# Pooling of k and v from the second batch on: accumulating transfers add the upper four of eight rows

## The chip, the cores and the metric

The kernel runs on one core of one Trainium2 chip. The metric is the device time of one execution in microseconds (us). Fewer is better.

## The reference, cut to what matters

Three stages follow one another, all in float32.

```
k_p = k.reshape(B, H, Sp, 8, D).mean(axis=3)      # k, v: (4, 8, 576, 64), Sp = 72
v_p = v.reshape(B, H, Sp, 8, D).mean(axis=3)
attn = softmax(q @ k_p^T / sqrt(64));  x = attn @ v_p        # 2304 tokens x 512
x = (silu(xn @ w_gate) * (xn @ w_val)) @ w_out               # xn = x / rms(x) * g, d_ff 1536
out = (x @ w_a) * (x @ w_b) @ w_out2                         # d_ff 1536
```

What is changed is the first two lines: each mean is over 8 rows of 64 numbers that lie side by side in memory, so that one pooled row is made of 512 contiguous numbers (2 KB). A batch has 576 such groups for k and 576 for v (8 heads of 72).

## The kernel before, in words

Tokens are worked on in tiles of 512, 256, 512, 512 and 512. In the first tile attention, the conversion of the weights and the first feed-forward run side by side; `FIRST` and `SECOND` (lines 32 to 52) are lists of tokens that give the order in which the steps are written for the first two tiles, and a list scheduler then places the instructions on each engine by its own estimate of when they are ready. Once placed, every engine works in that order, and an instruction that waits holds up all behind it on its engine. The same holds for SP, which issues all transfers. Each weight is loaded in 512 KB pieces (`st`, four buffers), scaled by ACT (L589, L590), given its sign by DVE (L596, L599) and completed by POOL (L606) into `wf`; a matrix product needs a rounded weight `wh` (ACT, L620) and its rest `wl` (POOL or DVE, L621). Products of the first tile are L791 (g and v) and L814 (`acc`); of later tiles L649 and L662. The bank of v is a single one: the next product v can't begin before DVE has read the last one (`ht`, L805 in the first tile, L1235 later).

`prep_steps(b)` pools k and v of batch b. `load` (L158) brings a piece of two chunks, each 72 rows (one head of k) or 128 rows (v) by 512 numbers; v ends in a chunk of 64 rows, so a batch has 7 pieces. Buffers are `kv`, two of them (the first batch has others besides). `pool_to` (L174) sums a chunk by `reduce_sum` over the 8 rows (DVE, L189, one instruction a chunk) or, where a token has an exclamation mark, a piece by three halving additions on POOL (L180 twice, L183), and then calls `load` for the next piece. In batch 1 seven chunks are summed by DVE and three pieces by POOL; in batches 2 and 3 DVE sums all 13 chunks. The pooled keys `kp` are transposed by PE (L210) and copied to `KB`; the pooled values `vp` are spread into `vm` (L228, L244) and split (`vh`, `vl`, L253, L254). The scores are L318, their maximum and difference L327 and L328, and `el` (L380) is the rest of the transposed weights of attention, which the product xT (L399) needs.

After the attention of the last tile, which is over at about 300 us, PE works through the rest of the first feed-forward and the whole second one.

Of the kernel before, what the change touches and what calls it, by code (L numbers as in the profile page):

```python
# [8 lines left out]
F32 = mybir.dt.float32  # L9
# [3 lines left out]
I64 = mybir.dt.int64  # L13
AF = mybir.ActivationFunctionType
ALU = mybir.AluOpType
AX = mybir.AxisListType

P = 128
# [45 lines left out]
def attention_moe_moe2(  # L64
# [14 lines left out]
    nc = tc.nc  # L79
    B, H, S, D = q.shape  # L80
    NT, DM = out.shape
    FF = w_gate.shape[1]
    POOL = 8
    SP = S // POOL
# [4 lines left out]
    NV = 5  # L89
# [12 lines left out]
    at_p = attn.enter_context(tc.tile_pool(name="at", bufs=2, side="right"))  # L102
# [9 lines left out]
    for t0, n in starts(TILES1):  # L112
# [9 lines left out]
        out=mask, in_=mask, pattern=[[P, NV], [-SP, H]], compare_op=ALU.is_ge,  # L122
# [3 lines left out]
        out=mask, in_=mask, pattern=[[-P, NV], [SP, H]], compare_op=ALU.is_ge,  # L126
# [3 lines left out]
    for i in range(2):  # L130
        t = const.tile([P, NP, 2 * SP], F32, tag=f"KB{i}", name=f"KB{i}")
# [10 lines left out]
    def att_bank(name, tag=None):  # L142
        if tag is not None:
            pass
        else:
            tag = boot["banks"].pop(0) if boot["banks"] else "att"
        return ps.tile([P, 512], F32, tag=tag, name=name, bufs=2 if tag == "att" else 1)

    def prep_steps(b):
        kf = k[b].rearrange("h (sp r) d -> (h sp) (r d)", r=POOL)  # L150
        vf = v[b].rearrange("h (sp r) d -> (h sp) (r d)", r=POOL)
        tail = HK - (NV - 1) * P
        pieces = [(kf[c * SP:(c + 2) * SP], SP) for c in range(0, H, 2)]
        pieces += [(vf[c * P:(c + 2) * P], P) for c in range(0, NV - 1, 2)]
        pieces += [(vf[(NV - 1) * P:], tail)]
        queue = []

        def load():  # L158
            if not pieces:
                return  # L160
            src, rows = pieces.pop(0)
            i = len(pieces)
            if boot["on"] and i not in (1, 4):
                t = st_p.tile([P, 512], I64, tag="st", name=f"kv_{b}_{i}")
            else:
                t = at_p.tile([P, 512], I64, tag="kv", name=f"kv_{b}_{i}", bufs=2)
            t = t.bitcast(F32).rearrange("p (c x) -> p c x", c=2)
            if rows == tail:
                nc.sync.dma_start(out=t[:rows, 0], in_=src)
            else:  # L170
                nc.sync.dma_start(out=t[:rows], in_=src.rearrange("(c p) x -> p c x", p=rows))
            queue.append((t, rows))

        def pool_to(dst, c0, on_pool=False):  # L174
            t, rows = queue.pop(0)
            nc_ = 1 if rows == tail else 2
            if on_pool:
                v4 = t[:rows, :nc_].rearrange("p c (r d) -> p c r d", r=POOL)
                for half in (4, 2):
                    nc.gpsimd.tensor_add(  # L180
                        v4[:, :, :half, :], v4[:, :, :half, :], v4[:, :, half:2 * half, :]
                    )
                nc.gpsimd.tensor_add(  # L183
                    dst[:rows, c0:c0 + nc_, :], v4[:, :, 0, :], v4[:, :, 1, :]
                )
                load()
                return
            for c in range(nc_):
                nc.vector.reduce_sum(  # L189
                    out=dst[:rows, c0 + c, :],  # L190
                    in_=t[:rows, c].rearrange("p (r d) -> p d r", r=POOL),
                    axis=AX.X,
                )
            load()

        box = {}

        def k_pool(c):
            if c == 0:
                box["kp"] = sm_p.tile([SP, H, D], F32, tag="kp", name=f"kp_{b}")  # L200
            pool_to(box["kp"], c, boot["alt"])

        def v_pool(c):
            pool_to(vp, c, boot["on"] or boot["alt"])

        def k_transpose():
            kb = KB[b % 2]
            kp, bank = box["kp"], att_bank(f"kT_{b}")
            for p in range(NP):
                nc.tensor.transpose(  # L210
                    bank[:, p * SP:(p + 1) * SP],
                    kp[:, 2 * p:2 * p + 2, :].rearrange("p a d -> p (a d)"),
                    ident[:SP, :SP],
                )
            for hh in range(2):
                rows = slice(hh * D, (hh + 1) * D)
                dst = kb[rows, :, hh * SP:(hh + 1) * SP]
                src = bank[rows, :NP * SP].rearrange("p (a s) -> p a s", a=NP)
                if hh == 0 and b == 0:
                    nc.scalar.mul(dst, src, 1.0 / POOL)  # L220
                else:
                    nc.vector.tensor_scalar_mul(dst, src, 1.0 / POOL)

        def v_mask():
            vm = at_p.tile([P, NP, 2, P], F32, tag="vh", name=f"vm_{b}")
            VM[b] = vm
            for pr in range(NP):
                nc.gpsimd.tensor_mul(  # L228
                    vm[:, pr].rearrange("p c (a d) -> p c a d", a=2),
                    vp[:, pr:pr + 2, :].unsqueeze(2).to_broadcast([P, 2, 2, D]),  # L230
                    mask[:, pr:pr + 2, 2 * pr:2 * pr + 2].unsqueeze(3).to_broadcast([P, 2, 2, D]),
                )

        def v_split(half):
            if half == 0:
                VH[b] = at_p.tile([P, NP, 2, P], F32R, tag="vh", name=f"vh_{b}")
                VL[b] = at_p.tile([P, NP, 2, P], F32R, tag="vl", name=f"vl_{b}")
            if b in VM:
                vm = VM[b][:, 2 * half:2 * half + 2].rearrange("p a c d -> p (a c d)")
            else:  # L240
                vm = ev_p.tile([P, 512], F32, tag="ev", name=f"vm_{b}_{half}")
                for i in range(2):
                    pr = 2 * half + i
                    nc.vector.tensor_mul(  # L244
                        vm[:, i * 256:(i + 1) * 256].rearrange("p (c a d) -> p c a d", c=2, a=2),
                        vp[:, pr:pr + 2, :].unsqueeze(2).to_broadcast([P, 2, 2, D]),
                        mask[:, pr:pr + 2, 2 * pr:2 * pr + 2].unsqueeze(3).to_broadcast(
                            [P, 2, 2, D]
                        ),
                    )  # L250
            dst_h = VH[b][:, 2 * half:2 * half + 2].rearrange("p a c d -> p (a c d)")
            dst_l = VL[b][:, 2 * half:2 * half + 2].rearrange("p a c d -> p (a c d)")
            nc.scalar.copy(dst_h, vm)  # L253
            nc.vector.tensor_sub(dst_l, vm, dst_h.bitcast(F32))  # L254

        loads = [load] * (6 if b == 0 else 2)
        steps = [lambda c=c: k_pool(c) for c in range(0, H, 2)]
        steps += [lambda c=c: v_pool(c) for c in range(0, NV, 2)]
        steps += [k_transpose]
        if b < 2:  # L260
            steps += [v_mask]
        if b > 0:
            steps += [lambda h=h: v_split(h) for h in range(2)]
        return loads, steps
# [416 lines left out]
    A = [score_steps(u) for u in range(NU)]  # L681
    V = [value_steps(u, dest(u)) for u in range(NU)]
    loads, prep = zip(*(prep_steps(b) for b in range(B)))

    nc.sync.dma_start(out=gneg, in_=rms_g.rearrange("(c p) -> p c", p=P))
# [615 lines left out]
```

## Time and profile before

| what | us |
|---|---|
| median of 3 runs (1028.54, 1029.00, 1031.03) | 1029.0 |
| the execution that was profiled | 1029.57 |
| its span, first to last instruction | 1027.8 |
| PE busy (95% of the span) | 978.7 |
| DVE busy (62%) | 638.3 |
| POOL busy (41%) | 417.3 |

PE is TensorE's matmuls, PEld its weight loads, DVE is VectorE, ACT ScalarE, POOL GpSimd, SP the engine that issues transfers. Times of a timeline are microseconds from the span's start. What stands in square brackets behind a row is how long the engine was idle before it, and what it waited for.

### The profile page before, as it was taken

How to read it: one execution, taken by the hardware profiler on the slowest of the kernel's cores; microseconds unless marked ns; L12 is line 12 of the kernel's file. 1: busy time of each engine (PE TensorE's matmuls, PEld its weight loads, DVE VectorE, ACT ScalarE, POOL GpSimd, SP SyncE). 2: the span in 40 equal slices, each digit the busy share in tenths (PEclk: the TensorE clock that was granted, in tenths of full speed). 3: DMA queues.
4: the chain of work that ended last, by engine and by line, in shares of the span. 5: the costliest groups of instructions: out<-in, count | busy, mean ns of one | idle time of the engine just before them, and what ended most of it. 6: DMA issues, size and time to landing. Idle time of an engine off the chain costs nothing. (4 is left out here: it accounts for less than half of the span.)

```text
span 1027.8 us, 13784 instructions
## 1 busy us (share of the span) xinstructions
PE 978.7 (95%) x4988; PEld 846.3 (82%) x4988; DVE 638.3 (62%) x994; ACT 463.4 (45%) x874; POOL 417.3 (41%) x332
## 2 busy tenths in 40 slices
PE   4978999989899999999999999999999999999998
PEld 3766666788788887888788889999999999888886
DVE  6898966997843756363627759766676665322221
ACT  2855662565454536444436545434444434331211
POOL 5476672546443434344357620533344332310000
PEclk8799999989999999999999999999999999999999
DMA  8556543330100002000102033444443434643431
GB/s 220 163 175 193 174 134 102 102 91 1 41 1 21 1 1 62 1 1 1 41 24 80 28 125 108 144 135 147 138 144 130 134 128 167 213 141 118 138 112 72
DMA packets 82803, 101.55 MB, mean 99 GB/s; under 512 B 24112, under 2 KB 63024, under 8 KB 82736
## 3 DMA queue, kind: packets, MB, share of 16 engines
q1 hardware_dynamic: 82736, 100.69, 31.5%
q8 instruction: 39, 0.64, 0.3%
q14 instruction: 28, 0.23, 0.1%
HBM read 73.93 MB, written 26.74 MB: 98 GB/s over the span
## 5 line engine op out<-in xcount | busy, mean ns | idle before, releaser
L621 POOL TENSOR_TENSOR wl<-wf,wh 128x512 fp32r<-128x512 f32 x156 | 214.1, 1382 | 236.0 <-ACT wh L620 234.0
L620 ACT CAST wh<-wf 128x512 fp32r<-128x512 f32 x168 | 102.0, 618 | 77.3 <-PE v L649 28.8
L1095 DVE TENSOR_TENSOR hl<-hf,hh 128x768 fp32r<-128x768 f32 x36 | 34.4, 961 | 95.7 <-ACT hh L1094 95.6
L1117 PE MATMUL o<-woh,hl 128*128 128x512 f32 x216 | 85.8, 397 | 0.0
L1117 PE MATMUL o<-woh,hh 128*128 128x512 f32 x216 | 85.0, 394 | 0.0
L1117 PE MATMUL o<-wol,hh 128*128 128x512 f32 x216 | 84.7, 392 | 0.0
L606 POOL TENSOR_TENSOR w<-w,st 128x512 int32<-128x512 int32 x24 | 31.9, 1329 | 115.4 <-DVE w L599 114.3
L662 PE MATMUL acc<-hh,wl 128*128 128x512 f32 (+1 forms) x192 | 70.6, 368 | 5.7 <-ACT hh L1238 5.7
L649 PE MATMUL v<-xh,wl 128*128 128x512 f32 (+1 forms) x192 | 72.7, 379 | 1.1 <-DVE ht L1235 0.9
L649 PE MATMUL g<-xh,wl 128*128 128x512 f32 (+1 forms) x192 | 71.4, 372 | 0.0
L662 PE MATMUL acc<-hl,wh 128*128 128x512 f32 (+1 forms) x192 | 70.1, 368 | 0.5 <-DVE hl L1239 0.3
L649 PE MATMUL g<-xh,wh 128*128 128x512 f32 (+1 forms) x192 | 70.6, 368 | 0.0
L1094 ACT CAST hh<-hf 128x768 fp32r<-128x768 f32 x36 | 29.8, 834 | 90.2 <-PE o L1117 82.5
L649 PE MATMUL g<-xl,wh 128*128 128x512 f32 (+1 forms) x192 | 70.2, 366 | 0.0
L649 PE MATMUL v<-xl,wh 128*128 128x512 f32 (+1 forms) x192 | 70.0, 365 | 0.0
L649 PE MATMUL v<-xh,wh 128*128 128x512 f32 (+1 forms) x192 | 69.8, 363 | 0.0
L662 PE MATMUL acc<-hh,wh 128*128 128x512 f32 (+1 forms) x192 | 69.7, 364 | 0.0
L606 POOL TENSOR_TENSOR wf<-wf,st 128x512 int32<-128x512 int32 x36 | 53.0, 1477 | 38.8 <-DVE wf L599 16.6
L1235 DVE TENSOR_TENSOR ht<-ht,v 128x512 f32<-128x512 f32 (+1 forms) x48 | 29.6, 616 | 48.0 <-PE v L649 42.5
L1024 ACT COPY p<-X 128x384 f32<-128x384 f32 x36 | 17.3, 480 | 90.1 <-PE X L1016 90.1
L1227 ACT ACTIVATE ht<-g 128x512 f32<-128x512 f32 (+1 forms) x48 | 26.1, 545 | 63.8 <-PE g L649 54.5
L1239 DVE TENSOR_TENSOR hl<-ht,hh 128x512 fp32r<-128x512 f32 (+1 forms) x48 | 43.0, 895 | 14.6 <-ACT hh L1238 13.7
(208 smaller groups left out, 2772.5 us busy)
## 6 DMA issues: line engine op xcount, KB each, us to landing
hf<-h SPq DMA_DIRECT2D x36, 384.0 KB
st<-in_moe_w_out_dram SPq DMA_DIRECT2D x24, 512.0 KB
h<-u SPq DMA_DIRECT2D x36, 192.0 KB
h<-p SPq DMA_DIRECT2D x36, 192.0 KB
st<-in_moe_w_gate_dram SPq DMA_DIRECT2D x12, 512.0 KB
st<-in_moe_w_val_dram SPq DMA_DIRECT2D x12, 512.0 KB
st<-in_moe_w_a_dram SPq DMA_DIRECT2D x12, 512.0 KB
st<-in_moe_w_b_dram SPq DMA_DIRECT2D x12, 512.0 KB
```

The source lines that it names most:

```text
L606: nc.gpsimd.tensor_tensor(out=bits, in0=bits, in1=low, op=ALU.add)
L620: nc.scalar.copy(wh, wf[ph, f, i])
L621: (nc.vector if boot["alt"] else nc.gpsimd).tensor_sub(wl, wf[ph, f, i], wh.bitcast(F32))
L649: nc.tensor.matmul(bank[:, :n], w[:, c, :], x[:, c, cols], start=(i == 0), stop=(i == 3 * KD - 1),)
L662: nc.tensor.matmul(accs[c][:, cols], w[:, c, :], x[:, :n], start=(f == 0 and i == 0 and cols.start == 0), stop=(f == NF - 1 and i == 2),)
L1024: nc.scalar.copy(t, src[:, :HALF])
L1094: nc.scalar.copy(hh, hf)
L1095: nc.vector.tensor_sub(hl, hf, hh.bitcast(F32))
L1117: nc.tensor.matmul(accs[i], x[:, sub], y, start=(f == 0 and j == 0), stop=(f == NF - 1 and j == 2),)
L1227: act = nc.scalar.activation(out=ht[:, :m], in_=gb[:, :m], func=AF.Silu)
L1235: nc.vector.tensor_mul(ht[:, :m], ht[:, :m], vb[:, :m])
L1239: low = nc.vector.tensor_sub(hl[:, :m], ht[:, :m], hh.bitcast(F32)[:, :m])
```

## The change

From batch 1 on (batch 0 stays as it was) k and v come in four groups rather than seven pieces: two of four heads of k, one of four chunks of v, and the rest of v. Of each group two transfers are made. SP brings the lower four of the eight rows (`r = 0`, 1 KB of each 2 KB), and when these have landed, a transfer issued by POOL brings the upper four and adds them in memory to the lower ones (`accum_op`). A chunk then has 256 numbers a row instead of 512, so that `reduce_sum` goes over four rows, and POOL makes two additions a piece instead of three. There are still two `kv` buffers, each now of four chunks. A table gives the turns of `load` at which each transfer is issued.

```diff
+        groups = [(kf[c * SP:(c + 4) * SP], 4, SP) for c in range(0, H, 4)]
+        groups += [(vf[:(NV - 1) * P], NV - 1, P), (vf[(NV - 1) * P:], 1, tail)]
+        held, turn = {}, [0]
+
+        def issue(g, r):
+            src, cnt, rows = groups[g]
+            if r == 0:
+                t = at_p.tile([P, 512], I64, tag="kv", name=f"kv_{b}_{g}", bufs=2)
+                held[g] = t.bitcast(F32).rearrange("p (c x) -> p c x", c=4)
+            (nc.gpsimd if r else nc.sync).dma_start(
+                out=held[g][:rows, :cnt],
+                in_=src.rearrange("(c p) x -> p c x", p=rows)[:, :, r * 256:(r + 1) * 256],
+                **({"accum_op": ALU.add} if r else {}),
+            )
+            if r:
+                queue.extend((held[g][:, c:c + 2], rows) for c in range(0, cnt, 2))
+
         def load():
+            if b > 0:
+                for g, r in (
+                    [(0, 0), (1, 0)], [(0, 1), (1, 1)], [], [(2, 0)], [], [(3, 0), (2, 1), (3, 1)],
+                    [], [], [],
+                )[turn[0]]:
+                    issue(g, r)
+                turn[0] += 1
+                return
...
+            n_r = POOL if b == 0 else POOL // 2
             if on_pool:
-                v4 = t[:rows, :nc_].rearrange("p c (r d) -> p c r d", r=POOL)
-                for half in (4, 2):
+                v4 = t[:rows, :nc_].rearrange("p c (r d) -> p c r d", r=n_r)
+                for half in (4, 2)[-(n_r // 4):]:
...
-                    in_=t[:rows, c].rearrange("p (r d) -> p d r", r=POOL),
+                    in_=t[:rows, c].rearrange("p (r d) -> p d r", r=n_r),
```

Lines below the new code have numbers that are 26 higher in the kernel after: L189 is L215, L180 is L206, L596 and L599 are L622 and L625, L606 is L632, L621 is L647, L805 is L831. The new transfers are all L167.

The scheduler places things anew. Three places show what moves. The first is on DVE in batch 1, at about 44 to 55 us of the span before; `kp` are the pooled keys, `br` and `by` the small steps to the reciprocal root of the second half of the first tile, `dg` its result. Before:

```order
L478 TENSOR_SCALAR ba_472<-sq_413 128x4
L189 TENSOR_REDUCE kp_605<-kv_6_568 72x64
L481 TENSOR_SCALAR br_473<-ba_472 128x4
L189 TENSOR_REDUCE kp_605<-kv_6_568 72x64
L636 TENSOR_TENSOR xl<-xf_296,xh 128x2x256 x2
L485 TENSOR_SCALAR br_473<-br_473 128x4
```

And after, further down:

```order
L517 TENSOR_TENSOR by_474<-br_473 128x4
L215 TENSOR_REDUCE kp_607<-kv_0_568 72x64
L518 TENSOR_TENSOR by_474<-by_474,ba_472 128x4
L625 SCALAR_TENSOR_TENSOR wf_0_2_562<-st_2_0_433,wf_0_2_562 128x512
L519 SCALAR_TENSOR_TENSOR br_473<-by_474,br_473 128x4
L831 TENSOR_TENSOR ht<-ht,v 128x256
L490 TENSOR_SCALAR dg_487<-ident,br_473 128x128 x2
L215 TENSOR_REDUCE kp_607<-kv_0_568 72x64
```

Of the two reductions that stood ahead of `dg` one is left there, later in the chain, and the other stands behind it.

The second place is again on DVE, at about 152 to 161 us, where the keys of batch 2 come in; `ht` is the read that frees the bank of v. Before:

```order
L599 SCALAR_TENSOR_TENSOR wf_0_11_1434<-st_11_2_1317,wf_0_11_1434 128x512
L410 TENSOR_TENSOR ss_1217<-ss_1217,sq_3_1314 128x256
L805 TENSOR_TENSOR ht<-ht,v 128x512
L478 TENSOR_SCALAR ba_1396<-sq_1393 128x4
L481 TENSOR_SCALAR br_1397<-ba_1396 128x4
```

After:

```order
L625 SCALAR_TENSOR_TENSOR wf_0_11_1431<-st_11_2_1314,wf_0_11_1431 128x512
L436 TENSOR_TENSOR ss_1214<-ss_1214,sq_3_1311 128x256
L215 TENSOR_REDUCE kp_1590<-kv_1_970 72x64 x4
L831 TENSOR_TENSOR ht<-ht,v 128x512
L504 TENSOR_SCALAR ba_1393<-sq_1390 128x4
L507 TENSOR_SCALAR br_1394<-ba_1393 128x4
```

Four reductions of the second group of keys of batch 2 now stand ahead of `ht`; before, the first reduction of batch 2 stood eighteen rows behind it.

The third place is on POOL in the same stretch; `DMA` rows are the accumulating transfers of batch 2. Before:

```order
L621 TENSOR_TENSOR wl_1364<-wf_0_11_1331,wh_1363 128x512
L606 TENSOR_TENSOR wf_0_11_1434<-wf_0_11_1434,st_11_2_1317 128x512
L621 TENSOR_TENSOR wl_1422<-wf_0_0_240,wh_1421 128x512
L621 TENSOR_TENSOR wl_1471<-wf_0_11_1350,wh_1470 128x512
L621 TENSOR_TENSOR wl_1570<-wf_0_1_435,wh_1569 128x512
```

After:

```order
L647 TENSOR_TENSOR wl_1361<-wf_0_11_1328,wh_1360 128x512
L632 TENSOR_TENSOR wf_0_11_1431<-wf_0_11_1431,st_11_2_1314 128x512
L167 DMA kv_0_968<-in_k_dram 72x4x256
L167 DMA kv_1_970<-in_k_dram 72x4x256
L647 TENSOR_TENSOR wl_1419<-wf_0_0_240,wh_1418 128x512
L647 TENSOR_TENSOR wl_1468<-wf_0_11_1347,wh_1467 128x512
L167 DMA kv_2_1609<-in_v_dram 128x4x256
L167 DMA kv_3_1637<-in_v_dram 64x256
L647 TENSOR_TENSOR wl_1567<-wf_0_1_435,wh_1566 128x512
```

Four transfers have come in between, two of them ahead of the first `wl` of the second tile.

## Rows read from the trace of the kernel before

**Rows 1.** Page, part 1: busy us, share of the span, instructions.

```profile
PE 978.7 (95%) x4988; PEld 846.3 (82%) x4988; DVE 638.3 (62%) x994; ACT 463.4 (45%) x874; POOL 417.3 (41%) x332
```

**Rows 2.** Table by stretch; after the times PEclk is the granted clock.

```profile
87.25:91.70 4.45, 4.45 (x13) 3.48 (x13) 4.42 (x6) 2.14 (x4) 2.29 (x2) 0.62 0.55 184
186.40:209.66 23.26, 18.23 (x148) 17.41 (x146) 20.84 (x28) 13.59 (x27) 13.42 (x10) 0.96 0.30 82
209.66:214.50 4.84, 4.84 (x22) 4.84 (x23) 4.84 (x7) 2.04 (x7) 2.55 (x2) 0.50 0.20 58
300.00:1000.00 700.00, 695.23 (x3496) 616.38 (x3495) 393.30 (x615) 297.77 (x561) 249.73 (x190) 1.00 0.28 91
```

**Rows 3.** Lines 189 and 180: durations of one, least, median, most.

```profile
L189 DVE TENSOR_REDUCE kp<-kv x26: 995/1060/1128, 6.1 to 220.1; 72x64 f32<-72x512 f32 x26
...
L180 POOL TENSOR_TENSOR kv<-kv x14: 717/1010/1722, 9.0 to 85.1; 72x512 f32<-72x512 f32 x3, 72x256 f32<-72x256 f32 x3, 128x512 f32<-128x512 f32 x3, 128x256 f32<-128x256 f32 x3
```

**Rows 4.** Timeline of DVE, two contiguous reductions: start, duration, engine, line.

```profile
109.20 0.44 DVE L327 TENSOR_REDUCE m<-sc 128x4 f32<-128x288 f32 x1
...
115.07 1.34 DVE L339 TENSOR_REDUCE sum<-e 128x16 f32<-128x1152 f32 x1
```

**Rows 5.** Page, part 3: the one queue that moves data, packets, MB, share.

```profile
q1 hardware_dynamic: 82736, 100.69, 31.5%
```

**Rows 6.** Timeline of SP, then of ACT: one weight load and its first reader.

```profile
146.37 0.34 SPq L571 DMA_DIRECT2D st<-in_moe_w_out_dram  x1
...
149.66 0.68 ACT L589 ACTIVATE wf<-st 128x512 f32<-128x512 f32 x1 [0.87 <-DMA st<-in_moe_w_out_dram]
```

**Rows 7.** Timeline of DVE, 44 to 56 us: in the first batch with new pooling.

```profile
44.56 1.09 DVE L189 TENSOR_REDUCE kp<-kv 72x64 f32<-72x512 f32 x1
...
48.21 0.16 DVE L491 TENSOR_TENSOR by<-br 128x4 f32<-128x4 f32 x1
...
49.97 1.29 DVE L491 TENSOR_TENSOR by<-br 128x4 f32<-128x4 f32 x1
51.18 0.68 DVE L599 SCALAR_TENSOR_TENSOR wf<-st,wf 128x512 int32<-128x512 int32 x1
...
54.76 0.83 DVE L464 TENSOR_SCALAR dg<-ident,br 128x128 f32<-128x128 f32 x2
```

**Rows 8.** Timeline of POOL, the gap in the same stretch.

```profile
49.78 1.46 POOL L606 TENSOR_TENSOR wf<-wf,st 128x512 int32<-128x512 int32 x1 [4.20 <-DVE br L493]
```

**Rows 9.** Timeline of PE, its waits for DVE between 55 and 88 us.

```profile
55.65 0.70 PE L472 MATMUL rb<-dg,ones 128*128 128x256 f32 x2 [2.00 <-DVE dg L464]
...
76.98 0.47 PE L791 MATMUL v<-xh,wl 128*128 128x512 f32 x1 [1.43 <-DVE ht L805]
...
87.25 0.50 PE L791 MATMUL v<-xh,wl 128*128 128x512 f32 x1 [2.79 <-DVE ht L805]
```

**Rows 10.** Timeline of DVE, then of POOL and PE, around 156 us.

```profile
160.02 0.69 DVE L805 TENSOR_TENSOR ht<-ht,v 128x512 f32<-128x512 f32 x1 [4.14 <-PE v L791]
...
155.56 1.49 POOL L606 TENSOR_TENSOR wf<-wf,st 128x512 int32<-128x512 int32 x1
...
161.19 0.39 PE L791 MATMUL v<-xh,wl 128*128 128x512 f32 x1
```

**Rows 11.** Timeline of PE, three later waits.

```profile
178.98 0.67 PE L472 MATMUL rb<-dg,ones 128*128 128x256 f32 x2 [1.38 <-DVE e L328]
...
202.18 0.36 PE L649 MATMUL v<-xh,wl 128*128 128x256 f32 x1 [0.86 <-DVE ht L1235]
...
209.66 0.58 PE L399 MATMUL xT<-el,vh 128*128 128x256 f32 x1 [3.94 <-DVE el L380]
```

**Rows 12.** Timeline of POOL, then of PE: a weight rest and its first reader.

```profile
175.50 1.28 POOL L621 TENSOR_TENSOR wl<-wf,wh 128x512 fp32r<-128x512 f32 x1 [13.14 <-ACT wh L620]
...
190.12 0.28 PE L649 MATMUL g<-xh,wl 128*128 128x256 f32 x1
```

## The prediction

> **What bounds the kernel now.** I read the busy shares first. PE is busy for 978.7 of 1027.8 us, DVE for 62% and POOL for 41% [rows 1]; so a change that takes work from DVE and POOL is worth only what it takes from PE's waits. Next I read the table by stretch. Between 300 and 1000 us PE is busy for 695.23 of 700 us at clock 1.00 [rows 2]: nothing is to be had there, and an earlier or later start of that part moves the end by the same amount. All pooling lies before it. Between 186 and 210 us, in contrast, PE works for 18.23 of 23.26 us and DVE for 20.84 [rows 2]: there PE waits for DVE. So I went on to PE's timeline and to its waits near each pooling. Batch 1 has three, of 2.00, 1.43 and 2.79 us [rows 9]. Batch 2 has none at 161.19, one of 1.38 at 178.98 and one of 0.86 at 202.18; at the beginning of the next tile's attention there is one of 3.94 [rows 10, 11]. A wait has an aftermath: after the one of 3.94 the granted clock is 0.50 for 4.84 us, after the one of 2.79 it is 0.62 for 4.45 us [rows 2]; the lower level is 1.2 of 2.4 GHz, so these cost 4.84 x 0.50 = 2.4 and 4.45 x 0.38 = 1.7 us more. The forecast is the sum over these places.
>
> **What is taken away.** DVE's reductions from batch 1 on are 7 + 13 + 13 = 33, at a median of 1.06 us [rows 3]. Of four rows the trace has none. Two contiguous reductions take 0.44 us for 288 numbers and 1.34 for 1152 [rows 4], that is 1.04 ns a number and 0.14 us fixed. If the fixed part is as large in the strided one, 512 numbers cost 0.92 us and 256 cost 0.46, in all 0.60. The bounds are 0.53 (half of all) and 1.06 (nothing gained). I take 0.60, since the fixed part is what the nearest rows show. DVE gets 33 x 0.46 = 15 us back; how much of that PE gets is the question below. POOL loses the larger first addition of three pieces in batch 1, up to 1.7 us each [rows 3]; it waits there anyway (4.20 us ahead of 49.78) [rows 8], so that I count nothing.
>
> **What is added.** Twelve transfers issued by POOL, and for each a wait on POOL until SP's transfer of the lower rows has landed. The trace has no transfer from POOL and none that adds: all 82736 packets are of SP's queue [rows 5]. So I bound it. To issue one costs POOL at least what it costs SP, 0.34 us [rows 6], and at most about its longest addition, 1.7 us [rows 3]; I take 1.0, the middle. From issue to landing: SP's 512 KB are there after 3.3 us (issue at 146.37, and the reader starts at 149.66 after waiting for it) [rows 6]. 288 KB by bytes alone are 1.9 us; reading also what it adds to, and longer besides, could make it twice 3.3, 6.6 us. I take 3.3, since that is the measured one. From POOL's arrival a single transfer is thus there after 4.3 us, the second of two after 5.3. Below nothing it can't be, for the reductions wait for the landing and no reader comes before it.
>
> The Trainium skill, "DMA: Bandwidth & Descriptors", section on the anatomy of one DMA on the gpsimd path, has a price: 2.0 us and the bytes by 436 KB/us, here 2.7 us; for 512 KB it gives 3.2, with which SP's 3.3 [rows 6] agrees. By it the forecast would come out about 2 us lower, at 1028, an estimate; no run here shows such a transfer that adds.
>
> **Batch 1 (45 to 90 us).** POOL reaches the two accumulates when its `wl` is over, at 44.30 + 1.28 = 45.58, at the head of a gap of 4.20 us [rows 8]. The first lands at 45.58 + 4.3 = 49.9. On DVE two reductions (1.09 + 1.05 = 2.14 us; the first is the one at 44.56) stood ahead of `dg`; one of 0.60 remains, later in the chain. DVE comes to it after the long `by`, which ended at 49.97 + 1.29 = 51.26 [rows 7], minus 2.14, plus three steps of 0.16: at 49.6. It waits 0.3 us, and `dg` comes 2.14 - 0.60 - 0.3 = 1.2 us earlier, which PE's wait of 2.00 [rows 9] can take in full. Four further reductions stand ahead of the `ht` of PE's waits of 1.43 and 2.79 [rows 9]; they give 4 x 0.46 = 1.84 us, of which I count half, 1.0, since the converted weights there also wait for their transfers. Batch 1: -2.2.
>
> **Batch 2 (155 to 165 us), where it may be lost.** POOL reaches its two accumulates when L606 ends, at 155.56 + 1.49 = 157.05 [rows 10]. The second lands at 157.05 + 5.3 = 162.35. On DVE all four reductions of this second group stand ahead of the `ht` that frees the bank of v. Before, DVE was idle for 4.14 us up to that `ht` at 160.02, and PE took the bank at 161.19 without waiting [rows 10]. Now DVE stands at the first reduction until 162.35, then needs 4 x 0.60 = 2.4 and 0.69 for `ht`: 165.4, and PE waits 165.4 - 161.2 = 4.2 us. That is longer than the wait of 3.94, so the clock falls after it; between 1.7 and 2.4 [rows 2] I take 2.0. In exchange the reductions are gone from ahead of `e`, and the wait of 1.38 at 178.98 [rows 11] goes. Batch 2: 4.2 + 2.0 - 1.4 = +4.8.
>
> **Between 195 and 215 us.** The wait of 0.86 goes with two shorter `vp` reductions (2 x 0.46 = 0.92) ahead of it. The 3.94 [rows 11] loses about two more, 0.92; the rest of 3.0 still lets the clock fall. -1.8.
>
> **The rest.** POOL's queue gets the two accumulates of v behind it in batch 2, one of which waits for a load that itself waits for the reductions; the `wl` that began at 175.50 would begin at up to 175.5 + 4.2 (the reductions are later by what PE waits) + 3.3 (that load) = 183.0, and its first reader stands at 190.12 [rows 12]: hidden. If it weren't, each us beyond 190.12 - 1.28 would be a us for PE. SP's later loads in batch 1 wait for the accumulates and their readers, with weight loads queued behind; that is why I counted half there.
>
> Sum: -2.2 + 4.8 - 1.8 = +0.8. The profiled execution took 1029.57; 1030.4, and as the median of the runs is 0.57 lower than that execution, **1029.8 us**.
>
> **Rivals.** (1) *The accumulates are quick* (0.34 + 1.9): the second is there at 157.05 + 0.68 + 1.9 = 159.6, `ht` ends at 162.7, PE waits 1.5 us, no more than waits it has without a fallen clock, and the 1.38 that goes pays for it. Batch 1 gives 2.14 - 0.60 + 1.84 = 3.4; with the 1.8 that is -5.1, thus 1024. For it speaks that 288 KB are few; against it, that the lower bound of both parts is needed at once. 0.27. (2) *The accumulates are slow* (1.7 + 6.6): in batch 2 the second is there at 157.05 + 3.4 + 6.6 = 167.05, `ht` ends at 170.1, PE waits 8.9 us, with the clock 2.4, less 1.4: +9.9. In batch 1 the first is there at 53.9, 4.3 us after DVE needs it: -1.54 + 4.3 - 1.0 = +1.8. The first reduction of batch 3, just ahead of the `el` that xT waits for, takes back the 1.8. Together +11.7, thus 1041. It decides from where issue and landing of the second together exceed about 6.5 us (each us is one of PE). For it speaks that POOL and DVE disturb one another: the same step `by` takes 0.16 us alone and 1.29 beside an L606 of POOL [rows 7, 8]. Against it, that around 157 us DVE is idle. 0.30. (3) *POOL stands at an accumulate until SP's load has landed, and `wl` comes late after all*: 7 us of slack [rows 12] speak against it; beyond that I'd expect 3 to 4 us, 1034. 0.05.
>
> On the second rival the Trainium skill, "SBUF — State Buffer", section "Who interferes with whom", says that DVE's copies and `tensor_scalar` can hold the port that GpSimd needs to write a transfer's descriptors, and that such a transfer then stalls. The two lengths of `by` agree that the engines share something; that a transfer suffers no run here shows. By this rule it is batch 1, where DVE has no pause, that would lose: +1.8 in place of -2.2, and 1034.
>
> **Chances.** The forecast 0.38, the rivals 0.27, 0.30 and 0.05. About 0.3%, 3.1 us, is what a measurement of this kernel tells from no change: 1025.9 to 1032.1. The forecast lies within it, the first rival below, the other two above. A reduction of 0.8 us instead of 0.60 makes batch 2 0.8 worse and the other places 1.4: still within it. Range 1023.5 to 1041, from the first rival to the second.
>
> **What would show it.** In the profile after: a second queue that moves data, issued by POOL; the time from POOL's issue to the first reduction, 4 to 5 us if I am right; reductions of 0.6 us; in batch 2 DVE idle at the first `kp` until about 162, waiting for a transfer, and then PE waiting for `ht` for about 4 us with a lower clock behind it; in batch 1 PE's wait for `dg` below 1 us. I am wrong if that wait of PE is missing (first rival) or 8 us long (second), or if PE loses time behind 300 us, where I count none.

## The result and the profile after

The changed kernel takes 1042.24 us in the median of four runs (1038.73 to 1045.41), the kernel before 1028.77 in the runs beside them: a ratio of 1.0126, interval 1.0106 to 1.0145, slower by some 13 us. The forecast was 1029.8, the range ended at 1041. The profiled execution is the fastest of the four, 1038.73 us with a span of 1037.0; against the profile before it shows 9.2 of the 13 us.

The page's busy shares and the queues that move data (packets, MB, share of 16 engines):

```profile
PE 983.1 (95%) x4988; PEld 849.6 (82%) x4988; DVE 625.8 (60%) x994; ACT 463.0 (45%) x874; POOL 425.8 (41%) x341
...
q1 hardware_dynamic: 82616, 97.15, 30.3%
q0 software_dynamic: 4224, 3.54, 2.4%
```

DVE is busy for 12.5 us less than in [rows 1], and the second queue, which [rows 5] did not have, is there. The instructions on `kv` (ns: least, median, most), and of POOL's transfers the median us from issue to landing:

```profile
L215 DVE TENSOR_REDUCE kp<-kv x26: 569/600/1029, 5.1 to 223.0; 72x64 f32<-72x256 f32 x20, 72x64 f32<-72x512 f32 x6
L215 DVE TENSOR_REDUCE vp<-kv x13: 589/610/639, 69.2 to 231.4; 128x64 f32<-128x256 f32 x10, 64x64 f32<-64x256 f32 x3
...
L167 POOL DMA_DIRECT2D kv<-in_k_dram x6: 1199/1311/1652, 44.2 to 216.0; - x6
...
kv<-in_k_dram POOLq DMA_DIRECT2D x6, 288.0 KB, 6.6
kv<-in_v_dram POOLq DMA_DIRECT2D x3, 512.0 KB, 5.9
```

The reduction over four rows takes 0.60 us, as forecast. To issue an accumulate of k costs POOL 1.3 us, near the 1.0 taken. From its issue a transfer does not take 3.3 us to land but 6.6 in the median for 288 KB of k and 5.9 for 512 KB of v. What that does in batch 2 stands on the timelines of POOL, DVE and PE (start, duration, engine, line, in brackets the idle time before and what ended it):

```profile
156.01 2.45 POOL L167 DMA_DIRECT2D kv<-in_k_dram  x2
...
165.23 2.06 DVE L215 TENSOR_REDUCE kp<-kv 72x64 f32<-72x256 f32 x4 [10.33 <-DMA kv<-in_k_dram]
167.21 0.67 DVE L831 TENSOR_TENSOR ht<-ht,v 128x512 f32<-128x512 f32 x1
...
167.93 0.79 PE L817 MATMUL v<-xh,wl 128*128 128x512 f32 x1 [7.53 <-DVE ht L831]
```

The reductions begin 165.23 - 156.01 = 9.2 us after POOL began to issue the pair; DVE stands still for 10.33 us, `ht` comes behind, and PE, which did not wait here before [rows 10], waits 7.53 us. Two stretches of the table by stretch, with the granted clock third from the end:

```profile
157.00:166.00 9.00, 3.40 (x17) 2.51 (x15) 0.77 (x2) 1.73 (x3) 3.96 (x4) 0.94 0.78 153
166.00:172.00 6.00, 4.07 (x9) 3.14 (x10) 4.24 (x18) 0.00 (x0) 0.68 (x1) 0.52 0.29 87
```

Behind the wait the granted clock is 0.52, nearly all the time at the lower level of 1.2 GHz. PE works for 4.07 of these 6 us (the wait reaches into them), so that costs 4.07 x 0.48 = 2.0 us more. The other places that the forecast spoke of, on PE's timeline:

```profile
53.14 1.22 PE L840 MATMUL acc<-ht,wf 128*128 128x256 f32 x2 [2.75 <-DVE ht L831]
...
76.03 0.60 PE L817 MATMUL v<-xh,wl 128*128 128x512 f32 x1 [2.27 <-DVE ht L831]
...
216.48 0.58 PE L425 MATMUL xT<-el,vh 128*128 128x256 f32 x1 [4.45 <-DVE el L406]
...
275.85 0.55 PE L688 MATMUL acc<-hh,wl 128*128 128x256 f32 x1 [4.34 <-ACT hh L1264]
```

Of the waits in [rows 9] the 2.00 for `dg` is gone, but a new one of 2.75 for `ht` stands just ahead of it; the 1.43 has become 2.27; the 2.79 is gone, and one of 1.81 for ACT's `ht` comes at 89.62. The waits of 1.38 and 0.86 in [rows 11] are gone or down to 0.36; the 3.94 has become 4.45. The last row is a mark: the same wait for `hh` stands at 268.19 in the kernel before. The xT starts 6.8 us later than before; from it to that mark it took 58.5 us before, now 59.4; from the mark to the end 759.6 and 761.2. That last stretch takes 759.6 to 762.5 us in the thirteen profiles behind this document, whose instructions are the same there, so the 1.6 us of it are within the scatter.

### The profile page after: what moved, and what is told of

Same layout as the page of the kernel before. It is cut to its first block, busy times and chain, and to the rows that moved or that the text cites. A ratio compares the mean times of both kernels' runs of the same rounds, so it can differ in the third digit from the quotient of the medians.

```text
span 1037.0 us, 13794 instructions
## 1 busy us (share of the span) xinstructions
PE 983.1 (95%) x4988; PEld 849.6 (82%) x4988; DVE 625.8 (60%) x994; ACT 463.0 (45%) x874; POOL 425.8 (41%) x341
## 3 DMA queue, kind: packets, MB, share of 16 engines
q0 software_dynamic: 4224, 3.54, 2.4%
## 4 chain that ended last, share of the span: by engine, by line
PE 76%; DVE 12%; DMA 4%; issue 3%; ACT 2%; POOL 1%; SPq 1%; DVEq 0%; ACTq 0%; POOLq 0%
PE o L1143 14%; PE X L1042 13%; PE g L675 10%; PE v L675 9%; PE acc L688 8%; PE Y L1042 6%; PE Z L1042 3%; PE acc L840 3%; DMA kv<-in_k_dram 2%; PE xT L425 2%; PE g L817 2%; PE v L817 2%; PE sc L344 2%; DVE wf L625 1%; DVE wf L622 1%
## 5 line engine op out<-in xcount | busy, mean ns | idle before, releaser
L647 POOL TENSOR_TENSOR wl<-wf,wh 128x512 fp32r<-128x512 f32 x156 | 214.3, 1389 | 212.7 <-ACT wh L646 209.2
L632 POOL TENSOR_TENSOR w<-w,st 128x512 int32<-128x512 int32 x24 | 31.9, 1329 | 116.5 <-DVE w L625 115.4
L632 POOL TENSOR_TENSOR wf<-wf,st 128x512 int32<-128x512 int32 x36 | 54.0, 1505 | 36.1 <-DVE wf L625 20.7
```

Source lines behind the costliest of these rows:

```text
L632: nc.gpsimd.tensor_tensor(out=bits, in0=bits, in1=low, op=ALU.add)
L647: (nc.vector if boot["alt"] else nc.gpsimd).tensor_sub(wl, wf[ph, f, i], wh.bitcast(F32))
```

## The experiments

All times are medians beside runs of the kernel before on the same chip (1029.3 to 1029.8); the ratio is to these.

**Is it the addition?** Same order of instructions on every engine, no addition:

```diff
-                **({"accum_op": ALU.add} if r else {}),
+                **({}),
```

> The changed kernel, with its upper rows still brought by POOL at the same places, but written over the lower ones and not added to them (the addition is left out). Every engine has the same order of instructions. Theory A (the adding in memory makes the transfers long): in batch 2 the time from the issue on POOL to the first of the four reductions, 9.2 us in the changed kernel, falls to about 4 to 5 us, PE's wait for ht of 7.53 us falls to about 3, and the run takes some 5 us less than the changed kernel, about 1036. Rival B (it is the queue that POOL issues: descriptors of 1 KB written by software, whatever they do): the time stays at 8 to 9 us, PE's wait at 7 to 8, the run within 2 us of the changed kernel, about 1041.

Measured: 1036.02 us, 1.0068 (1.0052 to 1.0085), 6 us below the changed kernel. Its queue, and batch 2 on POOL, DVE and PE:

```profile
q0 software_dynamic: 1200, 3.54, 1.2%
```

```profile
152.99 1.52 POOL L167 DMA_DIRECT2D kv<-in_k_dram  x2
...
161.70 2.06 DVE L215 TENSOR_REDUCE kp<-kv 72x64 f32<-72x256 f32 x4 [9.82 <-DMA kv<-in_k_dram]
...
164.41 0.79 PE L817 MATMUL v<-xh,wl 128*128 128x512 f32 x1 [7.02 <-DVE ht L831]
...
212.00 0.74 POOL L167 DMA_DIRECT2D kv<-in_k_dram  x1 [0.44 <-DVE hl L1265]
...
215.77 1.14 DVE L215 TENSOR_REDUCE kp<-kv 72x64 f32<-72x256 f32 x2 [1.31 <-DMA kv<-in_k_dram]
```

Adding costs 4224 packets in place of 1200 for the same bytes, twice the engines' time (2.4% and 1.2%), and on POOL 1.3 in place of 0.75 us to issue. But here, where it hurts, the pair still takes 161.70 - 152.99 = 8.7 us and PE still waits 7.02. Theory A falls for this wait. For the total it holds in part: the intervals are apart, so the addition costs something, but the wait accounts for half a microsecond of the 6. Where the rest is isn't settled: single stretches differ by more than that between profiles of one and the same order (from PE's wait at 76 us to that at 114 us it is 37.6 us in the changed kernel, 35.4 here, and 35.6 with late readers, where the additions are in and the order of that stretch is the same).

**Earlier accumulates.** `=M1` in the list of the first tile moves from behind `-A3.3` to ahead of `=g10a`:

```diff
-v9a =g10a -s9.0 v9b
+v9a =M1 =g10a -s9.0 v9b
...
-=A3.2 -A3.3 =M1 -h12
+=A3.2 -A3.3 -h12
```

> The changed kernel, with the two accumulates of batch 2's keys issued earlier on POOL, behind the third last block of weights rather than the last (some 25 us earlier); PE's order is unchanged. Theory C (the price of an accumulate hurts only where a reader stands in front of ht and waits): PE's wait of 7.53 us in front of v is gone, and with it its clock loss; the run is 8 to 9 us below the changed kernel, about 1033. Rival D (the transfers disturb wherever they stand, by POOL's time or by holding up SP's loads): it wins less than 4 us, about 1039, and new waits of PE appear between 120 and 160 us.

Measured: 1041.28, 1.0112 (1.0097 to 1.0127): nothing won.

```profile
129.91 2.44 POOL L167 DMA_DIRECT2D kv<-in_k_dram  x2
155.71 1.31 POOL L167 DMA_DIRECT2D kv<-in_v_dram  x1
...
138.21 2.12 DVE L215 TENSOR_REDUCE kp<-kv 72x64 f32<-72x256 f32 x4 [8.72 <-DMA kv<-in_k_dram]
164.47 1.08 DVE L215 TENSOR_REDUCE vp<-kv 128x64 f32<-128x256 f32 x2 [9.88 <-DMA kv<-in_v_dram]
...
166.20 0.80 PE L817 MATMUL v<-xh,wl 128*128 128x512 f32 x1 [5.50 <-DVE ht L831]
```

The scheduler moved the readers forward with the transfers. DVE now waits twice, 8.72 us at 138 and 9.88 us at 164, the second time for an accumulate of v that had not been in front of this `ht` before. PE waits 1.32 us for an `ht` at 141, behind the first, and 5.50 behind the second. Rival D gave the right total, but for another reason: it is again readers in front of an `ht` that cost.

**Late readers.** The same accumulates at the same places; one token changed, which puts the four reductions of kv_1 and two of v behind:

```diff
-A4.0 =r0 -r1 r2 -r3
+A4.0 =r0 -r1 -r2 -r3
```

> The changed kernel, with accumulates issued where they were, but the four reductions of batch 2's second half of keys (and the two of its values) placed behind the reads of the bank of v that they stood in front of. Theory C: PE's wait of 7.53 us goes, 8 us below the changed kernel, about 1034; the reductions find their data there. Rival D: the cost moves to other places (later accumulates wait for the buffers that are freed later, and the attention of the next tile waits for keys), and the run stays above 1038.

Measured: 1031.75, 1.0027 (1.0012 to 1.0042), 10 us below the changed kernel.

```profile
156.27 2.44 POOL L167 DMA_DIRECT2D kv<-in_k_dram  x2
...
168.03 0.58 DVE L215 TENSOR_REDUCE kp<-kv 72x64 f32<-72x256 f32 x1
...
208.35 0.58 PE L425 MATMUL xT<-el,vh 128*128 128x256 f32 x1 [4.73 <-DVE el L406]
```

No wait ahead of the first reduction, none of PE at the next v, and the xT of the next tile starts at 208.35. So theory C holds: three quarters of the loss are this one position in DVE's order. (The two reductions of v moved too, but behind them PE did not wait in the changed kernel.)

**One batch at a time.** With `if b == 1:`, `if b == 3:` and `if b == 2:` in place of `if b > 0:` (and `n_r` to match):

> Only batch 1 is pooled in the new way; batches 2 and 3 are as in the kernel before. Theory C: batch 1 by itself is within 1.5 us of the kernel before (its accumulates land while DVE has other work: in the trace of the changed kernel PE was 1.3 us ahead at 40 us and 0.9 ahead at 150), so 1028 to 1031. Rival E: batch 1 costs 3 us or more (its granted clock is 0.79 and 0.86 between 45 and 95 us in the changed kernel against 0.89 and 0.93 before), so 1032 or more.

Measured: 1029.72, 1.0003 (0.9991 to 1.0015). Batch 1 is worth nothing either way.

> Only batch 3 is pooled in the new way; batches 1 and 2 are as in the kernel before. With batch 1 alone at +0.4 us and the change with late reductions at +2.4 us, theory C leaves up to 1 or 2 us for batch 3: 1029 to 1031. Rival H (the lighter reductions of batch 3 give PE some of what I had expected between 195 and 215 us): 1027 to 1028, faster than the kernel before.

Measured: 1033.23, 1.0034 (1.0021 to 1.0047), some 3.5 us lost, more than either theory said. On POOL, DVE and PE:

```profile
211.59 1.20 POOL L167 DMA_DIRECT2D kv<-in_k_dram  x1
219.06 1.32 POOL L167 DMA_DIRECT2D kv<-in_v_dram  x1
...
216.73 0.59 DVE L215 TENSOR_REDUCE kp<-kv 72x64 f32<-72x256 f32 x1 [2.40 <-DMA kv<-in_k_dram]
217.24 0.41 DVE L406 TENSOR_TENSOR el<-eT,eh 128x256 fp32r<-128x256 f32 x1
...
224.96 2.20 DVE L215 TENSOR_REDUCE vp<-kv 128x64 f32<-128x256 f32 x4 [3.07 <-DMA kv<-in_v_dram]
227.05 0.43 DVE L1261 TENSOR_TENSOR ht<-ht,v 128x256 f32<-128x256 f32 x1
...
217.70 1.25 PE L344 MATMUL sc<-KB,qTs 128*128 128x144 f32 x8 [0.81 <-DVE el L406]
```

A single accumulate, 5.1 us (of k) and 5.9 us (of v) from issue to reader, and again what PE needs, an `el` and an `ht`, stands right behind the reader. In the kernel before these stretches of DVE had no wait for a transfer. PE waits 0.81 us behind the first and 0.85 at 230.12, neither of which it had before, and the stretch from the first xT to the mark for `hh` takes 61.3 us (58.5 before). That stretch differs between profiles: 59.4 in the changed kernel, whose profiled run is the fastest of its four, but 61.8, 62.8 and 66.3 in the runs with a lone, with earlier and with swapped accumulates, whose instructions stand there in the same order. What batch 3 costs is thus not the same in every execution.

> Only batch 2 is pooled in the new way, with the reductions where the changed kernel has them. If the loss is the wait in front of ht, this alone costs 9 to 10 us, 1038 to 1040, with a wait of PE of 7 to 8 us at about 160 to 168 us; if it takes all three batches (two buffers and one queue that carry over from batch to batch), 1033 or less.

Measured: 1036.21, 1.0057 (1.0036 to 1.0078). The wait is there by itself, 7.49 us:

```profile
168.53 0.80 PE L817 MATMUL v<-xh,wl 128*128 128x512 f32 x1 [7.49 <-DVE ht L831]
```

The profiled run is about 1038, the slowest of the four; the median lies 6.4 us above the kernel before, not 9 to 10. The three batches by themselves add up to 0.4 + 6.4 + 3.5 = 10.3 of 13 us; the rest is within the intervals.

**Why the pair takes 9 us: its order?** `[(0, 1), (1, 1)]` becomes `[(1, 1), (0, 1)]` for batch 2. (The queue of pieces turns with it, so that the two halves of that batch's heads of k change places.)

> The changed kernel, with the two accumulates of batch 2's keys issued in the other order, so that DVE's four waiting reductions read the first of the pair and not the second; every other instruction stands where it stood. Theory F (transfers of POOL's queue go one after the other, so that the second one pays for the first): DVE's reductions begin about 5 to 6 us after the issue instead of 9.2, PE's wait falls from 7.53 to about 4, the run takes 3 to 4 us less than the changed kernel, about 1038. Rival G (both share the transfer engines with SP's weight and q loads of those microseconds and land together): the reductions still begin 8.5 us or more after the issue, the run within 1 us of the changed kernel.

Measured: 1041.34, 1.0107 (1.0076 to 1.0137).

```profile
154.32 2.44 POOL L167 DMA_DIRECT2D kv<-in_k_dram  x2
...
163.67 2.06 DVE L215 TENSOR_REDUCE kp<-kv 72x64 f32<-72x256 f32 x4 [10.45 <-DMA kv<-in_k_dram]
```

9.35 us again, but this run does not test theory F. The pieces enter the queue in the order of the issues, so the reductions in front of `ht` again read the second of the pair: in the trace they wait for its semaphore and begin when it has landed (155.14 + 8.5), while the first was there at 162.4 (154.32 + 8.1). What the order is worth is seen in the landings themselves. First and second of the pair, each counted from its own issue, in the changed kernel and then in the run with earlier accumulates; the second is issued 0.82 us after the first:

```profile
kv<-in_k_dram POOLq DMA_DIRECT2D x1, 288.0 KB, 7.8
kv<-in_k_dram POOLq DMA_DIRECT2D x1, 288.0 KB, 8.4
...
kv<-in_k_dram POOLq DMA_DIRECT2D x1, 288.0 KB, 5.3
kv<-in_k_dram POOLq DMA_DIRECT2D x1, 288.0 KB, 7.5
```

In the changed kernel the first is there at 163.8 and the second at 165.2, 1.4 us later; in the run with earlier accumulates at 135.2 and 138.2, 3.0 us later. So the second does pay for the first, as theory F has it, but here with 1.4 of the 9.2 us, not with 3 to 4. A reader that waits for the first alone was not tried.

**A lone one.** The first accumulate of the pair is left out, the order is kept:

```diff
-            (nc.gpsimd if r else nc.sync).dma_start(
+            (b, g, r) == (2, 0, 1) or (nc.gpsimd if r else nc.sync).dma_start(
```

> The changed kernel without the first of the two accumulates of batch 2's keys (the upper rows of four heads of that batch are left out); the second, which the waiting reductions read, is then alone in POOL's queue; every engine keeps its order. Theory J (two accumulates at once share the transfer engines, so a pair takes nearly twice as long as a single one): the reductions begin 5 to 6 us after its issue, as single ones do behind 200 us, and PE waits 3 to 4 us instead of 7.53; the run is 3 to 4 us below the changed kernel, about 1038. Rival G (what delays it are SP's weight and q loads of the same microseconds): they still begin 8 us or more after the issue and the run stays within 2 us of the changed kernel.

Measured: 1041.14, 1.0115 (1.0089 to 1.0141). POOL, DVE, and what SP issued beside it:

```profile
154.05 1.21 POOL L167 DMA_DIRECT2D kv<-in_k_dram  x1
...
161.97 2.06 DVE L215 TENSOR_REDUCE kp<-kv 72x64 f32<-72x256 f32 x4 [9.03 <-DMA kv<-in_k_dram]
...
154.13 0.37 SPq L592 DMA_DIRECT2D st<-in_moe_w_b_dram  x1
154.55 0.50 SPq L309 DMA_DIRECT2D q<-in_q_dram  x1
```

7.9 us, as long as the first of the pair (7.8). A single one of the same size took 5.1 in batch 3, where SP had no weights to load, and the first of the earlier pair took 5.3, with no load of SP issued between 124.74 and 133.70. Rival G is the nearer: of the 9.2 us some 5 are a single accumulate in a quiet place, nearly 3 more come with SP's 512 KB of weights and the q load that are issued in the same half microsecond, and the last 1.4 with its twin. The packets agree: in the changed kernel SP's queue has the 16 engines for 62% of the microsecond from 157 and for all of the next two, and the first packet of POOL's queue comes at 159.8, 3.8 us after the issue; in the earlier run it comes at 131.7, 1.8 us after it. But the shares don't simply add up: without loads of SP the twin added 3.0, and the earlier pair still took 138.21 - 129.91 = 8.3 us. That it is SP's loads, and which of the two, was not tried by taking them away; the comparison is between places of the program.

**What the shorter reductions are worth.** No accumulates at all:

```diff
-            (nc.gpsimd if r else nc.sync).dma_start(
+            r or nc.sync.dma_start(
```

> The changed kernel without its twelve accumulating transfers (the upper four rows are left out of the means); the reductions over four rows and all else stay, though the scheduler moves some reductions forward. It is what the shorter reductions would be worth if the additions cost nothing. If DVE's 15 us are worth what the forecast counted (2.2 in batch 1, about 3.2 behind), it is 4 to 6 us faster than the kernel before, 1023 to 1025. Rival I (the time saved on DVE is lost again where DVE and POOL run side by side, and PE is bounded elsewhere): within 2 us of the kernel before, 1027 to 1030.

Measured: 1026.96, 0.9974 (0.9964 to 0.9985): 2.7 us faster than the kernel before, between both theories. With additions that cost nothing, and the order that the scheduler then makes, the change wins this much. On DVE and PE:

```profile
198.72 3.08 DVE L270 TENSOR_TENSOR vm<-vp,mask 128x256 f32<-128x256 f32 x4
...
204.13 0.58 PE L425 MATMUL xT<-el,vh 128*128 128x256 f32 x1 [3.90 <-DVE el L406]
```

Even here xT waits 3.90 us: shorter reductions do not shorten that wait.

**A version worth keeping?** Late readers with batches 2 and 3, and with batch 2 alone:

> Batches 2 and 3 in the new way with the late reductions of the earlier run, batch 1 as in the kernel before. If batch 1 is worth nothing either way, about 1031 (the same as with all three batches and late reductions); if batch 1 costs a little, 1030; a version faster than the kernel before (under 1026) would mean that batch 1's 14 seconds-long waits of DVE on POOL matter, which I don't expect.

Measured: 1031.08, 1.0025 (1.0005 to 1.0045), as with all three batches. (The last clause there is a slip; no wait in this kernel is of seconds.)

> Only batch 2 is pooled in the new way, with the late reductions; batches 1 and 3 are as in the kernel before. Late reductions with all three batches are at +2.5 us, batch 1 at +0.4 and batch 3 at +3.5, so if the places add up batch 2 gains about 1 us: 1028 to 1029, the same as the kernel before or just below. If the places don't add up (batch 3's accumulates were hurt by batch 2's order), about 1031.

Measured: 1029.26, 0.9995 (0.9985 to 1.0005): the places add up, but no gain is left. None of the kernels with accumulates beats the kernel before.

## Why the prediction was wrong, step by step

- **The reduction: right.** 0.60 us forecast, 0.60 and 0.61 measured. DVE's busy time fell by 12.5 us (15 forecast); in the run without accumulates by 10.5, to 627.8, and there PE got 2.7.
- **The accumulate's landing: the step that failed.** I took 3.3 us because SP's plain 512 KB took that, and 5.3 from POOL's arrival for the second of two. Measured are 9.2, above even the bound that I set for one (1.7 + 6.6 = 8.3) and near that for two (10.0). The forecast had the first of the two there after 4.3 us; it took 7.8, and the second 1.4 more, not 1.0. The smaller part of the mistake was to take the nearest measured transfer for one of another kind (another queue, with an addition): in a quiet place that costs 5.1 to 5.3 us. The larger part, some 2.5 us, is what the transfer takes longer at this place; as far as the comparison of places shows, it was to count it as if it were alone, though SP's loads of the same microseconds stood in the trace of before too. That cause is argued, not shown.
- **Batch 2: mechanism right, size wrong.** The place, the `ht` behind four waiting reductions and the fallen clock came as described: 4.2 us forecast for the wait, 7.53 measured; 2.0 for the clock, 2.0 measured. The wait of 1.38 went. By these parts +4.8 became 7.5 + 2.0 - 1.4 = 8.1; from PE's wait at 114 to the xT it takes 95.7 us before and 102.8 in the changed kernel, 7.2 more, and batch 2 alone cost 6.4. That it is one position in DVE's order the run with late readers shows (10 us).
- **Batch 1: -2.2 forecast, nothing measured** (1.0003). Of the two reductions ahead of `dg` one was left, and its accumulate had just landed (5.6 us after the issue at 44.19): the reduction at 49.77 has no wait for a transfer. But `dg` came only 0.6 us sooner, not 1.2: from `ba`, the first of the small steps, to `dg` DVE takes 9.7 us (43.34 to 53.01), before 10.3 (44.49 to 54.76). Some of these steps grow beside POOL. DVE and POOL of the changed kernel there:

```profile
46.00 0.15 DVE L519 SCALAR_TENSOR_TENSOR br<-by,br 128x4 f32<-128x4 f32 x1
...
47.97 1.26 DVE L519 SCALAR_TENSOR_TENSOR br<-by,br 128x4 f32<-128x4 f32 x1
...
49.77 0.64 DVE L215 TENSOR_REDUCE kp<-kv 72x64 f32<-72x256 f32 x1
...
51.10 1.65 DVE L519 SCALAR_TENSOR_TENSOR br<-by,br 128x4 f32<-128x4 f32 x1
...
47.52 1.69 POOL L632 TENSOR_TENSOR wf<-wf,st 128x512 int32<-128x512 int32 x1 [0.69 <-issue]
...
51.47 1.27 POOL L632 TENSOR_TENSOR wf<-wf,st 128x512 int32<-128x512 int32 x1
```

  The `br` step takes 0.15 us while POOL issues the pair; 1.26 and 1.65 beside POOL's L632. Before, other steps of the chain grew about as much (2.9 us in all, now 3.2). The forecast had this effect in [rows 7], but priced it only for the transfers. And `ht` now stands behind the last `br`, just ahead of `dg`, so that PE waits 2.75 us for it in place of the 2.00.
- **195 to 215 us: -1.8 forecast, nothing in the trace** (0.86 became 0.36, 3.94 became 4.45). What stands ahead of `el` and takes longest are four `vm` products, not the reductions. On DVE and POOL of the changed kernel:

```profile
209.69 4.54 DVE L270 TENSOR_TENSOR vm<-vp,mask 128x256 f32<-128x256 f32 x4
...
209.99 2.95 POOL L647 TENSOR_TENSOR wl<-wf,wh 128x512 fp32r<-128x512 f32 x2
```

  They take 4.54 us, with two `wl` of POOL beside them; 3.27 in the kernel before and 3.08 without accumulates, there too with `wl` beside part of them. I had taken the wait of 3.94 in [rows 11] to shrink with any shorter instruction ahead of it.
- **Batch 3: not in the sum.** I had it only as 'takes back the 1.8' within the second rival; alone it costs 3.5 us.
- **The rivals.** The second, slow accumulates, is what happened, at 0.30: it gave 1041 with a PE wait of 8.9 us. The range ended on its price, and the measured time lies 1.2 us outside: the price has 1.8 for batch 1, which cost nothing, and nothing for batch 3, which alone cost 3.5. Its reason was wrong in part: DVE was idle for 10 us while the pair was under way, so the rule weighed there, that of the Trainium skill ("SBUF — State Buffer", section "Who interferes with whom"), that work of DVE starves such a transfer, is not what delayed it here. What the section says of two engines, that a DVE step with two inputs in SBUF contends with a GpSimd step that reads it, agrees with the `br` and `vm` steps above.

## What to carry to other kernels

Moving an addition from a compute engine into a transfer takes it off the engine's busy time, and puts a latency of 5 to 9 us in front of each reader; before doing it, look at what stands behind each reader on its engine, and place readers 10 us or more behind the issue. A transfer's price is to be taken from its own kind and from its own moment: here a transfer took 7.8 us beside another queue's loads and 5.3 without them. And a shorter instruction on a busy engine is worth what the waits behind it show to be its doing: here 10.5 us of DVE were worth 2.7.

## What the runs showed of the hardware that was not expected

- An accumulating transfer of POOL's queue moves the same 3.54 MB in 4224 packets instead of 1200 and takes the transfer engines twice as long (2.4% and 1.2% of the span). Single ones of 288 KB land for their reader 5.1 us after the issue with the addition and 3.8 without (212.00 to 215.77), in a quiet place.
- Two transfers of this queue, issued one behind the other, land one behind the other: 7.8 and 9.2 us after the first issue beside SP's loads, 5.3 and 8.3 where SP issued none in the first 3.8 us.
- Two kernels with late readers scatter: 1028.8 to 1036.8 (all three batches) and 1027.9 to 1039.7 us (batches 2 and 3) in 12 runs each, against 1025.2 to 1028.2 without accumulates. With batch 2 alone it is 1027.3 to 1031.4 in 11 runs. Why was not tried.
